# A channel-attention and MLP kernel: first chunk loaded without a cast, idle matmuls in the load stage, w_out prepared without GpSimd, and the batch change's reciprocal cut in four

## Chip, cores and metric

One core of one Trainium2 chip. The metric is the device time of one execution in microseconds (us).

## The reference

```
q, k, v: (4, 6080, 256) float32;  tau = 1
qn = q / (||q|| over the 6080 rows + 1e-6);  kn likewise
s  = kn^T @ qn / tau            # 256 x 256 for each of 4 batches
a  = softmax(s, last axis)
x  = (v @ a)                    # 24320 x 256
h  = x @ w_in                   # 256 -> 2048
y  = gelu_tanh(h) @ w_out       # 2048 -> 256
```

## The kernel before

A batch first needs its Gram matrix G = q^T k and the column norms, then a 256x256 softmax eT, then AW = a @ w_in (scaled by the row sums). From then on it is v-blocks of 512 rows: `hp = AW^T vT`, gelu on ScalarE (ACT), and the product with w_out. That product uses 7 instead of 8 half-size products on sums of weights and sums of gelu outputs; VectorE (DVE) makes the sums and TensorE (PE) accumulates them. The Gram matrix of the next batch is computed in between, pair by pair. For these later batches exp is made as (1 + tanh)/(1 - tanh), which is where the long reciprocal stands. Each block has eight pairs p = 0..7. Twelve blocks make a batch.

Names in the profile lines: `G` is the Gram matrix, `ss` a column sum of squares, `rk` and `dg` the factors 1/|k|, `S` the scaled scores, `eT` the softmax's numerators, `hp` and `g` a block's values before and after gelu, `wst` and `wcomb` w_out as loaded and as prepared, `r`, `p` and `q` accumulators of products, `c` a sum that DVE makes of two of them, `ot` the result that DVE transposes (its "turn"). An eviction is the copy of a finished product out of PE's accumulator. Code below is cut.

The load stage of batch 0 (all its q and k must be there before anything else can start):

```python
for c in range(nch):                     # chunks of 8, 7, 8, 8, 8, 6, 2 row groups
    if c >= 2:
        load_qk(0, c)                    # GpSimd queue, casts float32 to bf16
    if c >= 1:
        ss_rows(c - 1, 0); ss_rows(c - 1, 1)   # column sums of squares, on PE
    squares(0, c); fold_rows(0, c)       # ACT and DVE
    if c == nch - 1:
        ss_rows(c, 0); q_factor()
    for i in range(len(rows_of(0, c))):
        gram_row(0, c, i)
    if c == nch - 1:
        ss_rows(c, 1)
# ... loads of w_in, v, w_out ...
warm(14); scores(0); pe_vt(0, "r"); first_aw()   # idle matmuls, softmax, v transposed, AW
```

The weights' sums, in the first two blocks, and the loop at a batch change:

```python
def prep_wout(step):                     # step 0, 1 in block 0; 2 in block 1
    if step == 0:
        nc.gpsimd.tensor_copy(wc(A11), w_half(0, 0))
        nc.gpsimd.tensor_copy(wc(A12), w_half(0, 1))
        nc.gpsimd.tensor_scalar_mul(wc(NA22), w_half(1, 1), -1.0)
        nc.vector.tensor_add(WF[0], w_half(1, 0), w_half(1, 1))
        nc.vector.tensor_copy(wc(S1), WF[0])
        ...
# in the loop over blocks n and pairs p (cut):
    mm1(n, p)                            # hp and gelu
    mm2(n - 1, p)                        # products of the block before
    if p == 7: sums_2(n, 0, 4)           # three DVE sums
    if blk == 9:
        if p == 5: k_row(nxt)            # DVE: 1/norms, dg = diag(1/|k|)
        if p == 7: k_row_pe(nxt)         # PE: ones @ dg, then S on DVE
    if blk == 10:
        if p == 1: scores_b(nxt); scores_c(nxt)    # tanh; one 128x512 reciprocal; eT
        if p == 6: row_sums(nxt)                   # PE, reads eT
    if blk == 11:
        aw_part(nxt, p // 2, p % 2, "act" if p % 2 else "dve")
```

## Time and profile before

| | before |
|---|---|
| time, median of 3 runs | 727.25 us (726.23 to 728.44) |
| the profiled run | 728.82 us, span of the core 726.9 us |
| PE busy | 692.1 us |
| idle PE before 40 us / 40 to 75 / 75 to 700 / after | 16.2 / 3.5 / 9.4 / 5.8 us |
| first hp matmul | 41.45 us |

PE is busy 95% of the span.

### The profile page before, as it was taken

To read this page: it belongs to the slowest core of one execution; us is meant where nothing else is said; L and a number is where in the kernel's file an instruction comes from. 1 tells how busy PE (TensorE), PEld (TensorE's weight loads), DVE (VectorE), ACT (ScalarE), POOL (GpSimd) and SP (SyncE) were. 2 spreads that over 40 slices of the span, in tenths; PEclk is the share of its full clock that TensorE was granted. 3 is DMA by queue.
4 is the path that set the end of the run, shared out by engine and by line. 5 is a ranking of instruction groups with operands and counts; after the bars stand their busy time and mean duration, and the time that the engine had idled before them with its cause. 6 is when DMAs were issued, how large, how long until landed. Compare 5 with 4: busy or idle time off the path is not lost.

```text
span 726.9 us, 12069 instructions
## 1 busy us (share of the span) xinstructions
PE 692.1 (95%) x4752; PEld 469.7 (65%) x4840; DVE 509.0 (70%) x892; ACT 482.0 (66%) x589; POOL 76.5 (11%) x136
## 2 busy tenths in 40 slices
PE   4698999999999999999999999999999999999996
PEld 3555666666666666666666666666666666666665
DVE  3479787875866777788675878787686465564665
ACT  3275766776667667767666776677666767666673
POOL 4251101110001101110000110111000000000000
PEclk9899999999999999999999999999999999999999
DMA  9994897883349777875545887897334636556233
GB/s 175 201 249 78 134 138 115 134 133 57 59 67 156 116 130 136 137 109 87 86 73 83 140 139 121 124 143 115 57 60 72 99 59 99 77 80 94 42 59 55
DMA packets 161705, 77.87 MB, mean 107 GB/s; under 512 B 149408, under 2 KB 152736, under 8 KB 160928
## 3 DMA queue, kind: packets, MB, share of 16 engines
q0 software_dynamic: 14224, 40.51, 34.8%
q1 hardware_dynamic: 146944, 36.47, 31.0%
q8 instruction: 38, 0.62, 0.3%
q10 hardware_dynamic: 480, 0.11, 0.1%
q14 instruction: 19, 0.16, 0.1%
HBM read 78.91 MB, written 36.57 MB: 159 GB/s over the span
## 4 chain that ended last, share of the span: by engine, by line
PE 88%; DVE 5%; DMA 4%; issue 1%; ACT 1%; POOL 0%; DVEq 0%; POOLq 0%
PE hp L395 41%; PE r L489 23%; PE p L489 11%; PE q L489 5%; PE G L192 5%; DMA t<-in_k_dram 2%; PE ps L371 2%; DVE dn L348 1%; DMA t<-in_q_dram 1%; DVE c L505 1%; DVE aw L378 1%; DVE wf_a L442 1%; DVE t L460 0%; ACT th L340 0%; ACT g L399 0%
## 5 line engine op out<-in xcount | busy, mean ns | idle before, releaser
L399 ACT ACTIVATE g<-hp 128x1024 bf16<-128x1024 f32 (+1 forms) x384 | 387.9, 1015 | 203.9 <-PE hp L395 192.2
L395 PE MATMUL hp<-vT,aw 128*128 128x512 bf16 (+1 forms) x1363 | 354.4, 376 | 2.6
L489 PEld LDWEIGHTS <-wcomb 128*128 128x128 bf16 x2688 | 262.8, 98 | 107.1 <-issue 9.1
L395 PEld LDWEIGHTS <-aw 128*128 128x128 bf16 x1536 | 149.9, 98 | 109.0 <-issue 1.7
L489 PE MATMUL r<-t,wcomb 128*128 128x256 bf16 (+1 forms) x1152 | 148.6, 272 | 7.1 <-DVE c L505 6.8
L192 PE MATMUL G<-t 128*128 128x256 bf16 (+1 forms) x384 | 71.3, 289 | 14.6 <-DMA t<-in_k_dram 14.6
L505 DVE TENSOR_TENSOR c<-r,y 128x256 f32<-128x256 f32 (+1 forms) x95 | 39.9, 420 | 50.9 <-PE r L489 46.8
L505 DVE TENSOR_TENSOR c<-q,x 128x256 f32<-128x256 f32 (+1 forms) x48 | 20.2, 420 | 72.7 <-PE q L489 70.9
L473 DVE TENSOR_TENSOR t<-t,g 128x1024 bf16<-128x1024 bf16 (+1 forms) x96 | 65.0, 677 | 0.0
L472 DVE TENSOR_TENSOR t<-g 128x1024 bf16<-128x1024 bf16 (+1 forms) x96 | 64.9, 676 | 0.0
L471 DVE TENSOR_TENSOR t<-g,t 128x1024 bf16<-128x1024 bf16 (+1 forms) x96 | 63.4, 660 | 0.0
L111 POOL DMA_DIRECT2D vb<-in_v_dram x45 | 22.8, 507 | 356.3 <-PE hp L395 356.3
L513 DVE STREAM_TRANSPOSE ot<-c 128x256 f32<-128x256 f32 (+1 forms) x144 | 57.6, 425 | 1.9 <-DVE c L505 0.2
L144 ACT ACTIVATE sq<-t 128x1536 bf16<-128x1536 bf16 (+3 forms) x30 | 45.6, 1520 | 19.7 <-DMA t<-in_q_dram 16.6
L460 DVE TENSOR_TENSOR t<-g 128x2048 bf16<-128x2048 bf16 (+1 forms) x48 | 57.7, 1203 | 0.0
L192 PEld LDWEIGHTS <-t 128*128 128x128 bf16 (+1 forms) x384 | 39.3, 103 | 27.4 <-issue 10.2
L489 PE MATMUL r<-g,wcomb 128*128 128x256 bf16 (+1 forms) x384 | 49.3, 271 | 1.2
L489 PE MATMUL p<-t,wcomb 128*128 128x256 bf16 (+1 forms) x384 | 49.3, 271 | 1.1 <-DVE wcomb L443 1.1
L489 PE MATMUL p<-g,wcomb 128*128 128x256 bf16 (+1 forms) x384 | 49.3, 271 | 0.0
L489 PE MATMUL q<-g,wcomb 128*128 128x256 bf16 (+1 forms) x384 | 49.3, 271 | 0.0
L513 DVE STREAM_TRANSPOSE ot<-r 128x256 f32<-128x256 f32 (+1 forms) x48 | 21.4, 445 | 29.7 <-PE r L489 29.7
L145 DVE TENSOR_TENSOR sq<-t 128x1536 bf16<-128x1536 bf16 (+4 forms) x31 | 29.8, 961 | 15.0 <-DMA t<-in_k_dram 14.7
(95 smaller groups left out, 332.8 us busy)
## 6 DMA issues: line engine op xcount, KB each, us to landing
out_dram<-ot SPq DMA_DIRECT2D x176, 128.0 KB, 2.9
vb<-in_v_dram POOLq DMA_DIRECT2D x41, 256.0 KB, 5.2
t<-in_q_dram POOLq DMA_DIRECT2D x22, 384.0 KB, 5.2
t<-in_k_dram POOLq DMA_DIRECT2D x22, 384.0 KB, 4.4
t<-in_q_dram POOLq DMA_DIRECT2D x4, 512.0 KB, 12.5
t<-in_k_dram POOLq DMA_DIRECT2D x4, 512.0 KB, 13.5
wst<-in_moe_w_out_dram POOLq DMA_DIRECT2D x2, 1024.0 KB, 10.0
out_dram<-ot SPq DMA_DIRECT2D x12, 112.0 KB, 2.6
```

The costliest lines, as they stand in the source:

```text
L144: nc.scalar.activation(sq[:, 0:n, 0:256], qt[:, 0:n, :], AF.Square)
L145: nc.vector.tensor_mul(sq[:, 0:n, 256:512], kt[:, 0:n, :], kt[:, 0:n, :])
L192: nc.tensor.matmul(G[b][:, jc, :], lhsT=qt[:np_, r, jc * 128 : jc * 128 + 128], rhs=kt[:np_, r, :], start=first and jc == 0, stop=last and ...
L395: mm = nc.tensor.matmul(hp[:, u, :cols], lhsT=AW[b][:, cc, fc * 128 : fc * 128 + 128], rhs=vt_tiles[n][:, cc, :cols], start=cc == 0, stop= ...
L399: nc.scalar.activation(GS[n][:, 2 * p : 2 * p + 2, :cols], hp[:, :, :cols], AF.Gelu_apprx_tanh)
L460: nc.vector.tensor_sub(t1[:, :, :hc], quarter(n, 0, 1), quarter(n, 0, 0))
L471: nc.vector.tensor_sub(v[2], b22, v[1])
L472: nc.vector.tensor_sub(v[3], b22, quarter(n, 0, 1, f0, f1))
L473: nc.vector.tensor_sub(v[4], v[2], quarter(n, 1, 0, f0, f1))
L489: nc.tensor.matmul(ACCS[n, acc][:, :hc], lhsT=wcomb[:, w, fc, :], rhs=x, start=first and fc == 0, stop=fc == 7, skip_group_check=True)
L505: nc.vector.tensor_add(CS[n][:, tj, ci, :hc], ACCS[n, acc][:, :hc], XS[n, name][:, :hc])
L513: nc.vector.transpose(OT[n][:, tj * nb : tj * nb + nb, ci, :], src.rearrange("p (x t) -> p x t", t=32))
```

## The change

The intent is to shorten every place where PE waits: start the load earlier by two hardware queues, keep the clock up during the load, take the preparation of w_out off GpSimd (while GpSimd works on it, a DVE sum takes 3.78 instead of 1.21 us), and cut the one long reciprocal so that DVE can serve PE in between. The transposes of v's first block also move ahead of the softmax. The diff is cut.

```diff
+    def load_first():           # q by the SP queue, k by the ACT queue, float32, no cast
+    def cast_first(st):         # q cast on ACT, k on DVE
-        load_qk(0, 0)
+        first = load_first()
         load_qk(0, 1)
+        load_qk(0, 2)
+        WARM = [0, 6, 10, 12, 14, 14, 0]
+            if 1 <= c < nch - 1:
                 ss_rows(c - 1, 0)
                 ss_rows(c - 1, 1)
+                warm(WARM[c])                       # idle matmuls
-        warm(14); scores(0); pe_vt(0, "r"); first_aw()
+        pe_vt(0, "r"); warm(14); scores(0); first_aw()   # both vT copies now on DVE
+                if (f, ic) == (0, 1): nc.scalar.activation(o, i, AF.Copy, scale=...)
-            nc.gpsimd.tensor_copy(wc(A11), ...)  (and A12, NA22)
+            nc.vector.tensor_copy(wc(A11), w_half(0, 0))
+        if step == 2: nc.scalar.activation(wc(A12), w_half(0, 1), AF.Copy)
+        if step == 3: nc.scalar.activation(wc(NA22), w_half(1, 1), AF.Copy, scale=-1.0)
     def scores_c(b, step):      # four pieces of 128x128; eT behind the fourth
+        nc.vector.reciprocal(piece, piece)
                     if blk == 9:
-                        if p == 5:
+                        if p == 7:
                             k_row(nxt)
-                        if p == 7:
-                            k_row_pe(nxt)
                     if blk == 10:
+                        if p == 0:
+                            k_row_pe(nxt)
                         if p == 1:
                             scores_b(nxt)
-                            scores_c(nxt)
-                        if p == 6:
+                        if p in (2, 4, 6, 7):
+                            scores_c(nxt, (2, 4, 6, 7).index(p))
+                    if blk == 11:
+                        if p == 0:
                             row_sums(nxt)
-                        aw_part(nxt, p // 2, p % 2, "act" if p % 2 else "dve")
+                        aw_part(nxt, p // 2, p % 2, "act" if p in (1, 4, 5, 6) else "dve")
```

More of the change, by code (lines that the diff above doesn't have):

```diff
@@ L98, in load_one @@
         qk_tiles.setdefault((b, c), []).append(t)
+    def load_first():
+        r0, n = chunks_of(0)[0]
+        assert not with_rest(0, 0)
+        st = gp.tile([128, 2, n, 256], FP32, tag="g", name="qk_f32")
+        for which, eng in ((0, nc.sync), (1, nc.scalar)):
+            eng.dma_start(out=st[:, which], in_=(q, k)[which][0, 0 : R * 128, :].rearrange(
+                "(p r) c -> p r c", r=R)[:, r0 : r0 + n, :])
+        return st
+    def cast_first(st):
+        for which in range(2):
+            t = qkp.tile([128, 8, 256], BF16, tag="qk"[which], name=f"first{which}")
+            for h in range(2):
+                if which == 0:
+                    nc.scalar.activation(t[:, h * 4 : h * 4 + 4], st[:, 0, h * 4 : h * 4 + 4], AF.Copy)
+                else:
+                    nc.vector.tensor_copy(t[:, h * 4 : h * 4 + 4], st[:, 1, h * 4 : h * 4 + 4])
+            qk_tiles.setdefault((0, 0), []).append(t)
     def load_qk(b, c):
@@ L267, in pe_vt @@
         nc.vector.tensor_copy(vT[:, 0, :], ps[:, 0, :])
-        if n == 0:
-            nc.scalar.activation(vT[:, 1, :], ps[:, 1, :], AF.Copy)
-        else:
-            nc.vector.tensor_copy(vT[:, 1, :], ps[:, 1, :])
+        nc.vector.tensor_copy(vT[:, 1, :], ps[:, 1, :])
         vt_tiles[n] = vT
@@ L292, in first_aw @@
             for ic in range(2):
-                nc.vector.tensor_scalar_mul(AW[b][:, ic, f * 256 : f * 256 + 256],
-                                            ps[ic][:, f * 256 : f * 256 + 256], rs[:, ic : ic + 1])
+                o = AW[b][:, ic, f * 256 : f * 256 + 256]
+                i = ps[ic][:, f * 256 : f * 256 + 256]
+                if (f, ic) == (0, 1):
+                    nc.scalar.activation(o, i, AF.Copy, scale=rs[:, ic : ic + 1])
+                else:
+                    nc.vector.tensor_scalar_mul(o, i, rs[:, ic : ic + 1])
     def warm(n):
@@ L341, in scores_b, with scores_c @@
         TH[b] = th
-    def scores_c(b):
-        th = TH.pop(b)
-        dn = smx.tile([128, 2, 256], FP32, tag="S")
-        nc.vector.tensor_scalar(dn, th, -1.0, 1.0, op0=ALU.mult, op1=ALU.add)
-        nc.vector.reciprocal(dn, dn)
-        eT = smx.tile([128, 2, 256], BF16, tag="eT")
-        nc.vector.scalar_tensor_tensor(eT, th, 1.0, dn, op0=ALU.add, op1=ALU.mult)
-        ET[b] = eT
+    def scores_c(b, step):
+        th = TH[b]
+        if step == 0:
+            dn = smx.tile([128, 2, 256], FP32, tag="S")
+            DN[b] = dn
+            nc.vector.tensor_scalar(dn, th, -1.0, 1.0, op0=ALU.mult, op1=ALU.add)
+        dn = DN[b]
+        piece = dn[:, step // 2, step % 2 * 128 : step % 2 * 128 + 128]
+        nc.vector.reciprocal(piece, piece)
+        if step == 3:
+            eT = smx.tile([128, 2, 256], BF16, tag="eT")
+            nc.vector.scalar_tensor_tensor(eT, th, 1.0, dn, op0=ALU.add, op1=ALU.mult)
+            ET[b] = eT
+    DN = {}
     def row_sums(b):
@@ L438, in prep_wout @@
                 WF.append(t)
-            nc.gpsimd.tensor_copy(wc(A11), w_half(0, 0))
-            nc.gpsimd.tensor_copy(wc(A12), w_half(0, 1))
-            nc.gpsimd.tensor_scalar_mul(wc(NA22), w_half(1, 1), -1.0)
+            nc.vector.tensor_copy(wc(A11), w_half(0, 0))
             nc.vector.tensor_add(WF[0], w_half(1, 0), w_half(1, 1))
@@ L448, in prep_wout @@
         if step == 2:
+            nc.scalar.activation(wc(A12), w_half(0, 1), AF.Copy)
+        if step == 3:
+            nc.scalar.activation(wc(NA22), w_half(1, 1), AF.Copy, scale=-1.0)
+        if step == 4:
             nc.vector.tensor_sub(wc(S3), w_half(0, 0), w_half(1, 0))
@@ L618 @@
         nch = len(chunks_of(0))
+        WARM = [0, 6, 10, 12, 14, 14, 0]
         for c in range(nch):
-            if c >= 2:
+            if c == 0:
+                cast_first(first)
+            if c >= 3:
                 load_qk(0, c)
-            if c >= 1:
+            if 1 <= c < nch - 1:
                 ss_rows(c - 1, 0)
                 ss_rows(c - 1, 1)
+                warm(WARM[c])
             squares(0, c)
             fold_rows(0, c)
+            if c == nch - 2:
+                ss_rows(c, 0)
             if c == nch - 1:
@@ L629 @@
                 q_factor()
+                ss_rows(c - 1, 1)
             for i in range(len(rows_of(0, c))):
@@ L642 @@
         load_v0(2)
+        pe_vt(0, "r")
         warm(14)
         scores(0)
-        pe_vt(0, "r")
         first_aw()
@@ L660 @@
                 gate = mm1(n, p)
+                if n == 1 and p in (0, 3):
+                    prep_wout(2 + p // 3)
                 if p == 0 and n + 3 < NN:
@@ L673 @@
                         if n == 1:
-                            prep_wout(2)
+                            prep_wout(4)
                     if p == PAIRS - 1:
@@ L698 @@
                             norms(nxt)
-                        if p == 5:
+                        if p == 7:
                             k_row(nxt)
-                        if p == 7:
+                    if blk == 10:
+                        if p == 0:
                             k_row_pe(nxt)
-                    if blk == 10:
                         if p == 1:
                             scores_b(nxt)
-                            scores_c(nxt)
-                        if p == 6:
+                        if p in (2, 4, 6, 7):
+                            scores_c(nxt, (2, 4, 6, 7).index(p))
+                    if blk == 11:
+                        if p == 0:
                             row_sums(nxt)
-                    if blk == 11:
-                        aw_part(nxt, p // 2, p % 2, "act" if p % 2 else "dve")
+                        aw_part(nxt, p // 2, p % 2, "act" if p in (1, 4, 5, 6) else "dve")
         mm2_last(NN - 1)
```

## The prediction

> **What bounds the kernel now.** I first read the page's busy line, then who PE waits for, then the granted clock in short stretches, then the timelines of PE and DVE around each wait.
>
> ```profile
> PE 692.1 (95%) x4752; PEld 469.7 (65%) x4840; DVE 509.0 (70%) x892; ACT 482.0 (66%) x589; POOL 76.5 (11%) x136
> ```
>
> TensorE is busy 692.1 of 726.9 us, and the change removes no TensorE work of size. So all it can win lies in the 35 us of idle time and in stretches at half clock. By the table of stretches, 16.2 us of the idle time lies before 40 us, 3.5 us between 40 and 75 us, 9.8 us between 75 and 700 us, 5.8 us in the tail. The waits of PE:
>
> ```profile
> PE G L192 <- DMA t<-in_k_dram: 14.6, 4, 8.9
> PE r L489 <- DVE c L505: 6.8, 10, 1.9
> PE ss L210 <- DVE a L156: 1.6, 3, 0.7
> PE p L489 <- DVE wcomb L443: 1.1, 1, 1.1
> ```
>
> The first row is the load of q and k: the softmax of batch 0 needs all 12.5 MB, and the DMA engines show a share of about 1.0 from 4 us on. The second row has ten waits: one of 1.94 us at 64.49 us, and 0.33 + 0.87 + 0.42 = 1.62 us at each of three batch changes (183.83, 196.36, 211.58 us and their repeats); 1.94 + 3 x 1.62 = 6.8. The row of 1.1 is the wait for the summed weights at 54.77 us. The clock, in stretches of 3.41 us:
>
> ```profile
> 21.28:24.70 3.42, 2.00 (x24) 1.66 (x23) 1.22 (x1) 1.65 (x1) 1.45 (x2) 1.00 1.07 214
> 24.70:28.11 3.41, 1.42 (x18) 0.90 (x16) 1.23 (x1) 1.91 (x1) 0.70 (x1) 1.00 1.06 211
> 28.11:31.52 3.41, 2.05 (x10) 1.43 (x10) 1.94 (x2) 0.19 (x1) 0.71 (x1) 0.50 1.06 207
> ...
> 62.25:65.66 3.41, 1.47 (x16) 1.17 (x15) 3.28 (x6) 1.68 (x2) 0.53 (x1) 1.00 0.47 53
> 65.66:69.07 3.41, 3.41 (x17) 1.88 (x15) 2.87 (x7) 0.77 (x1) 0.00 (x0) 0.50 0.34 67
> ```
>
> The second column is PE's busy time, the third from the end the granted clock. A stretch with 1.42 or 1.47 us busy is followed by one at 0.50, one with 2.00 us busy is not. So the wait of 1.94 us is paid twice: the half clock after it costs about 3.41 / 2 = 1.7 us. What DVE does before these two waits:
>
> ```profile
> 49.71 3.78 DVE L442 TENSOR_TENSOR wf_a<-wst,wst 128x1024 f32<-128x1024 f32 x1
> 53.53 1.18 DVE L443 CAST wcomb<-wf_a 128x1024 bf16<-128x1024 f32 x1
> 54.63 1.21 DVE L444 TENSOR_TENSOR wf_a<-wf_a,wst 128x1024 f32<-128x1024 f32 x1
> ...
> 57.02 0.68 DVE L447 CAST wcomb<-wf_a 128x1024 bf16<-128x1024 f32 x1
> ```
>
> The same sum takes 3.78 us while GpSimd works on w_out (49.34 to 54.16 us) and 1.21 us alone, and the same cast 1.18 against 0.68. DVE then runs full until 65 us.
>
> **What the Trainium skill says.** (1) "SBUF — State Buffer", section "Who interferes with whom": a DVE instruction with two SBUF inputs contends with a GpSimd instruction that reads SBUF, and whoever comes first holds the pair for its whole instruction. The trace agrees (3.78 against 1.21). (2) "TensorE: Matmul & The Clock Gate", Part 1: the clock is halved or full, decided over free-running windows of 3413 ns. The length agrees: full speed ends at 28.11 and 65.66 us, 11 x 3.413 apart. The page asks for an idle window; here a window that was 42% busy was enough. (3) "DMA: Bandwidth & Descriptors", Specifications: first byte after about 0.6 us by hardware queue, 1 us by software queue; no run yet shows the first here. The "Key Constraints" of "Trainium Kernel Development and Optimization" say that all queues share the same 16 engines, so the new queues add no bandwidth. (4) "VectorE: DVE Perf Modes", "First, the fixed hardware budget": reciprocal is an iterative divide. The trace: 128x512 in 3.35 us and 128x4 in 0.18, so 6.24 ns an element; four pieces cost about what one does.
>
> **Part 1, the load.** The casting loads write 205 GB/s of bf16, which is 410 GB/s read; the fp32 loads of w_out at 42 to 47 us ran at 320 to 379 GB/s. So 2.1 MB of first chunk without the cast takes 5.8 instead of 5.1 us, 0.7 us more. Against it stands the start: between 2 and 4 us only 61 and 106 GB/s were written, 1.2 us worth of full rate lost, and the first issue waited for GpSimd until 1.23 us. I give 1.3 us back. The load ends about 0.6 us earlier. The first chunk itself lands later (three queues share the engines) and needs a cast, but PE has time to spare: chunks arrive every 5 us and need 3 to 4 us of work.
>
> **Part 2, idle matmuls.** They keep the clock full at 28 to 35 us, which alone would gain about 1 us at the last chunks. But they cost PE time where it counts: the fold of chunk 4 ends at 32.04, its sums end at about 32.75, 14 idle matmuls (0.109 us each, 1.53) end at 34.28, chunk 5's 12 Gram matmuls at 35.9, the rest about 37.5. Before, all of it ended at 37.60. So this part gives 0.1 us, and with Part 1 the head gains 0.7 us. The AW eviction on ScalarE gives nothing: the first hp starts at 41.45 us, when PE has just finished the ps matmuls (40.59 to 41.47), not when DVE has.
>
> **Part 3, w_out.** DVE now does A11 (0.68), the sum (1.21), S1 (0.68), the difference (1.2): S1 is ready at 49.75 + 2.6 = 52.3 instead of 54.7, before PE asks at 53.7. That removes 1.07 us. All of DVE's later work moves 2.4 us earlier. ScalarE takes A12 and -A22, 1.0 us each by the gelu of the same size (1.02); it has 0.6 to 0.9 us free per pair there and PE does not wait for it. At the product that waited 1.94 us PE now arrives 1.07 earlier and DVE 1.9 earlier (the sum is at 62.15 instead of 64.4, less the ends of pipelines): about 0.7 us of wait stay, PE is then 80% busy in that window, and the half clock goes. Gain: 1.07 + 1.24 + 1.7 = 4.0 us.
>
> **Part 4, batch changes.** Here I step through both engines in program order with the durations of the trace (hp 0.87, a product 0.87, three sums of half a block 1.77, c 0.34, L460 1.14). What goes: 0.33 (the k row no longer between two c), 0.87 (the long reciprocal), 0.42 (the AW eviction at p = 4 goes to ScalarE). What comes:
>
> ```profile
> 185.28 0.65 DVE L471 TENSOR_TENSOR t<-g,t 128x1024 bf16<-128x1024 bf16 x1
> 185.85 0.68 DVE L472 TENSOR_TENSOR t<-g 128x1024 bf16<-128x1024 bf16 x1
> 186.45 0.69 DVE L473 TENSOR_TENSOR t<-t,g 128x1024 bf16<-128x1024 bf16 x1
> ```
>
> These three stand at the end of every block, right behind the turn of r. The k row moves behind them: turn 0.37, sums 1.77, k row 0.87, some 0.2 of latency, 3.2 us after product 4; PE needs 3 x 0.87 = 2.6 to reach the matmul that reads it. A new wait of 0.6 to 0.7. One block later the fourth piece (0.9) and eT (0.7) stand behind the same sums: 0.4 + 0.37 + 1.77 + 0.9 + 0.7 = 4.1 us after product 4, and the row sums, moved to p = 0 of the next block, are reached after 2.6. A new wait of 1.5. Sum per batch change: 0.7 + 1.5 - 1.62 = +0.6, three times +1.8 us. A stall of 1.5 us leaves a window at least 56% busy, beside the 58% that did not drop and the 43% that did; I allow 0.3 us in all for a lost clock.
>
> **Sum:** -0.7 - 4.0 + 1.8 + 0.3 = -2.6, so 727.25 becomes 724.6 us.
>
> **Rivals.** (a) The batch changes work as meant: all 1.62 us go, three times, and the new waits do not come, because DVE does the sums or the pieces faster than I add up. For it: DVE is idle 0.6 us before the k matrices in my schedule. Against it: program order is fixed, and eT stands behind the sums. Then -0.7 - 4.0 - 4.9, 717.6 us. (b) The new wait of 1.5 us drops the clock each time: +1.7 three times, about 729.5. For it: the threshold lies between 43 and 58% of a window. Against: the wait must fall wholly into one window. (c) The DMA bounds the head and the hardware queues slow it (0.7 us more and a poorer start), and DVE stays the bound behind w_out with the clock still dropping: only 1.5 of the 4.0 come, 728.5.
>
> **Range and chances.** The stages are independent: head -1.5 to +0.7, w_out -5 to -2, batch changes -4 to +5. The low end 719.5 takes most of (a), the high end 729.0 is (b) or (c) nearly whole. 2% is 14.5 us; the whole removable idle time named here is 1.07 + 1.94 + 1.7 + 4.9 = 9.6 us, so faster by 2% has 0.01, and slower by 2% 0.01.
>
> **What would show it.** Right: no wait for wcomb and under 1 us for c at 60 to 70 us with the clock at 1.00; the 128x1024 sum at 1.2 us; new rows of PE waiting for dg (0.7, three times) and for eT at the row sums (1.5, three times); rows of c at batch changes gone; hp starting at 40.5 to 41.3 us. Wrong: no wait at the row sums (Part 4 fails), half clock at 190 to 205 us (b), first hp later than 41.5 us or half clock at 60 to 70 us (c).

## The result, and the profile after

726.11 us (median of 4 runs, 725.94 to 726.32) beside 726.79 us for the kernel before (4 runs, 726.23 to 728.44). Ratio 0.9987, 95% interval 0.997 to 1.0005: the same. Ratios here are the mean time of one kernel's fast runs over that of the other's of the same rounds, so they are not quite the ratio of the medians. The profiled run took 726.32 us, its span 724.6 us. The busy line of the page, and then who PE waits for (total us, times, longest us):

```profile
PE 693.5 (96%) x4808; PEld 472.0 (65%) x4896; DVE 508.8 (70%) x904; ACT 486.0 (67%) x593; POOL 70.2 (10%) x131
```

```profile
PE ps L386 <- DVE eT L377: 4.4, 3, 1.5
PE ps L350 <- DVE dg L344: 1.8, 3, 0.6
...
PE r L520 <- DVE c L536: 0.7, 1, 0.7
PE vt_ps L285 <- DMA v<-in_v_dram: 0.5, 1, 0.5
```

The ten waits for c (6.8 us) and the one for wcomb (1.1 us) have become one of 0.7 us. In their place stand three for eT and three for dg, one of each at each batch change. Stretches of the new trace around 65 us, columns as in the prediction:

```profile
58.81:62.22 3.41, 2.71 (x19) 1.70 (x18) 3.38 (x6) 3.41 (x5) 0.53 (x1) 1.00 0.22 43
62.25:65.66 3.41, 3.31 (x31) 2.48 (x30) 2.97 (x7) 1.59 (x2) 0.00 (x0) 1.00 0.78 115
65.66:69.07 3.41, 3.22 (x21) 1.93 (x21) 3.34 (x7) 2.25 (x3) 0.51 (x1) 1.00 0.07 12
```

The wait of 0.7 us that is left ends at 61.95 us and so falls into the first of them, which is still 79% busy. The second holds 3.31 us of busy time where before held 1.47 in the same stretch, and the clock stays at 1.00. DVE's timeline during the w_out sums:

```profile
50.22 1.22 DVE L469 TENSOR_TENSOR wf_a<-wst,wst 128x1024 f32<-128x1024 f32 x1
51.48 0.69 DVE L470 CAST wcomb<-wf_a 128x1024 bf16<-128x1024 f32 x1
```

These were 3.78 and 1.18 us. Adding up the two traces, by the starts of the same PE instructions:

| stage | before | after | difference |
|---|---|---|---|
| start to first hp | 41.45 | 41.40 | -0.05 |
| first hp to the first hp of block 2 | 29.28 | 25.38 | -3.90 |
| from there to the first product of 224 columns (first batch change in it) | 146.51 | 147.37 | +0.86 |
| from one such product to the next (second; the third alike) | 172.24 | 172.81 | +0.57 |
| the same product in the last batch to the end | 11.39 | 11.05 | -0.34 |

The sum, with the third batch change, is -2.3, which is what the two spans differ by. Of the +0.86, 0.30 us lie at the very start of block 2, where its first product follows the first hp after 1.16 us instead of 0.86; so w_out brings -3.6, and the first batch change costs 0.56 like the others. So w_out and the batch changes did roughly what the prediction said, the head did not, and in the two profiled runs the whole is -2.5 us of device time against a forecast of -2.6. Yet the medians differ by 0.7 only. Two questions are left: why the medians show less, and how much of this is really due to each part.

### The profile page after: what moved, and what is told of

It is laid out like the page before. It is cut to its first block, busy times and chain, and to the rows that moved or that the text cites. A ratio compares the mean times of both kernels' runs of the same rounds, so it can differ in the third digit from the quotient of the medians.

```text
span 724.6 us, 12205 instructions
## 1 busy us (share of the span) xinstructions
PE 693.5 (96%) x4808; PEld 472.0 (65%) x4896; DVE 508.8 (70%) x904; ACT 486.0 (67%) x593; POOL 70.2 (10%) x131
## 3 DMA queue, kind: packets, MB, share of 16 engines
q10 hardware_dynamic: 624, 1.16, 0.5%
## 4 chain that ended last, share of the span: by engine, by line
PE 87%; DVE 6%; DMA 4%; issue 1%; POOL 1%; ACT 0%; DVEq 0%; POOLq 0%
PE hp L424 41%; PE r L520 22%; PE p L520 11%; PE q L520 6%; PE G L213 4%; DMA t<-in_k_dram 2%; DMA v<-in_v_dram 2%; PE ps L400 2%; DVE ot L544 1%; DVE dn L374 1%; DVE t L504 1%; DVE t L502 1%; DVE t L503 1%; DVE c L536 0%; POOL t L93 0%
## 5 line engine op out<-in xcount | busy, mean ns | idle before, releaser
L213 PE MATMUL G<-t 128*128 128x256 bf16 (+1 forms) x368 | 64.8, 273 | 1.1 <-DMA t<-in_k_dram 1.1
L165 ACT ACTIVATE sq<-t 128x1536 bf16<-128x1536 bf16 (+3 forms) x29 | 43.7, 1506 | 9.8 <-DMA t<-in_q_dram 9.8
L213 PEld LDWEIGHTS <-t 128*128 128x128 bf16 (+1 forms) x368 | 35.5, 98 | 11.2 <-issue 2.7
L529 ACT ACTIVATE y<-p 128x256 f32<-128x256 f32 (+1 forms) x95 | 36.3, 382 | 0.7 <-ACT x L529 0.4
```

Source lines behind the costliest of these rows:

```text
L165: nc.scalar.activation(sq[:, 0:n, 0:256], qt[:, 0:n, :], AF.Square)
L213: nc.tensor.matmul(G[b][:, jc, :], lhsT=qt[:np_, r, jc * 128 : jc * 128 + 128], rhs=kt[:np_, r, :], start=first and jc == 0, stop=last and ...
L529: nc.scalar.activation(x[:, :hc], ACCS[n, acc][:, :hc], AF.Copy)
```

## The experiments

The parts were cut out of the diff and put on the kernel before one at a time (e1 to e3), or taken back from the changed kernel (e6, e7), and the batch changes were reordered (e4).

### e1: only w_out

```diff
-            nc.gpsimd.tensor_copy(wc(A11), w_half(0, 0))   # and A12, NA22
+            nc.vector.tensor_copy(wc(A11), w_half(0, 0))
+        if step == 2: nc.scalar.activation(wc(A12), w_half(0, 1), AF.Copy)
+        if step == 3: nc.scalar.activation(wc(NA22), w_half(1, 1), AF.Copy, scale=-1.0)
```

> The kernel before with the w_out part alone (A11 on DVE, A12 and -A22 on ScalarE, none on GpSimd). Theory: the waits of 1.07 and (1.94 - 0.70) us go, 2.3 us, and 1.7 us more in those runs of before that have a half-clock stretch at 65 us; so 722.9 to 724.5 beside 726.8. Rival, given back later: the time is within 0.7 us of before, with new PE waits after 75 us.

724.96 us (724.27 to 725.25, 6 runs) beside 726.3 (725.79 to 730.31, 11 runs); ratio 0.9964 (0.994 to 0.9988). This is a gain of 1.3 us by the medians, short of the 2.3 us that the theory asked for at the least. The rival fails too: it asked for less than 0.7 us and for new waits later. Why less than the 2.3 us of waits? In this run the clock was full at the last chunks, the first hp came at 39.98 us instead of 41.45, and DVE then had to wait for w_out itself:

```profile
49.28 1.23 DVE L440 TENSOR_TENSOR wf_a<-wst,wst 128x1024 f32<-128x1024 f32 x1 [0.39 <-DMA wst<-in_moe_w_out_dram]
```

From the first hp to that of block 2 it takes 25.87 us, beside 25.38 in the changed kernel and 27.44 in e2, which has the old w_out code and no half clock there. So against a full clock this part gains 1.6 us, not the 3.6 of the two profiled runs.

### e2: only the batch changes

```diff
  kernel before, with scores_c in four steps and the loop's lines for blk 9, 10, 11 taken from the change
```

> The kernel before with the batch-change part alone (k row later, reciprocal in four pieces, row sums a block later, AW evictions split differently). Theory: at each of three batch changes waits of 0.60 (dg) and 1.47 (eT) come and 1.62 go, so +0.45 to +0.6 each, 728.1 to 728.6 beside 726.8. Rival, pieces help as meant and the loss seen in the trace comes from the rest of the change: 722 to 725.

727.77 us (727.51 to 730.91, 6 runs): five of the six runs lie at 727.5 to 728.0. Beside the same runs of before as e1 that is 1.5 us more by the medians; the ratio, 1.0013 (0.9983 to 1.0042), has an interval that takes in 1, because before's mean holds its slower runs. The rival (722 to 725 us) failed. The trace has the same waits as the whole change (eT 4.4, dg 1.8 us) and 172.80 us from one product of 224 columns to the next, against 172.24 before. The loss at the batch change belongs to this part, not to the rest of the change.

This trace also settles something else. It still has the old w_out code and so the wait at 62 us, 1.95 us long, but no half clock follows it. PE's timeline, then the stretches between two window boundaries (its own clock returned to full at 27.5 us; 61.62 and 65.03 are 10 and 11 times 3.413 us later):

```profile
62.71 1.03 PE L496 MATMUL r<-t,wcomb 128*128 128x256 bf16 x8 [1.95 <-DVE c L512]
```

```profile
61.62:65.03 3.41, 2.32 (x22) 1.81 (x22) 2.97 (x6) 0.53 (x1) 0.00 (x0) 1.00 0.78 120
58.20:61.62 3.42, 2.56 (x17) 1.56 (x16) 3.39 (x7) 2.78 (x3) 0.53 (x1) 1.00 0.59 103
```

The wait lies across a boundary. Each window keeps 68 to 75% of busy time, and none is answered by half clock. In the profiled run of before the same wait lay inside one window (43% busy) and cost 1.8 us more: first hp to block 2 took 27.44 us here and 29.28 there. e3, which keeps the old w_out code too, agrees: its wait of 1.9 us leaves the two windows that it touches 79 and 64% busy, and the clock stays at 1.00.

### e3: only the head

```diff
  kernel before, with load_first, cast_first, the chunk loop, WARM, the vT order and the AW eviction taken from the change
```

> The kernel before with everything of the change up to the first hp (hardware-queue load, idle matmuls, vT of block 0 before the softmax, one AW eviction on ScalarE). Theory: last sums end 0.9 us earlier, but the vT copies stand before S on DVE and give all of it back; first hp at 41.4 us, time within 0.4 us of before. Rival: the head is worth the 0.7 us that the whole change gained, 726.1.

726.8 us (726.5 to 727.76, 6 runs), ratio 0.9994 (0.997 to 1.0019). The first hp came at 40.96 us, better than foreseen and yet 0.9 to 1.0 us later than in e1 and e2, which have the old head. By the medians it is 0.5 us slower than before, a little outside the 0.4 us of the theory; the rival's 726.1 did not come. So the head is no gain over an old head with full clock.

### e4: batch changes reordered

```diff
-                        if p == 7:
+                        if p == 6:
                             k_row(nxt)
-                        if p in (2, 4, 6, 7):
-                            scores_c(nxt, (2, 4, 6, 7).index(p))
+                        if p in (2, 3, 4, 6):
+                            scores_c(nxt, (2, 3, 4, 6).index(p))
```

> The changed kernel with the k row one pair earlier (p = 6, ahead of the block's last sums) and the reciprocal's pieces at p = 2, 3, 4, 6 instead of 2, 4, 6, 7, so that eT too stands ahead of those sums. Theory, only the order on DVE is at fault: the waits for dg (3 x 0.60) and eT (3 x 1.47) go, 6.2 us, 719.9 beside 726.1. Rival, DVE is short of time there whatever the order: the waits move to c or to the product that reads the half-block sums, 723 or more.

718.28 us (718.08 to 718.53, 6 runs), ratio to before 0.9874 (0.985 to 0.9897): 1.6 us below the theory, and far from the rival. Not one wait for eT or dg is left in PE's list of waits. In the changed kernel DVE's timeline behind the turn of r, at the end of block 10, was this:

```profile
196.68 0.68 DVE L504 TENSOR_TENSOR t<-t,g 128x1024 bf16<-128x1024 bf16 x1
197.28 0.94 DVE L374 RECIPROCAL dn<-dn 128x128 f32<-128x128 f32 x1
198.25 0.69 DVE L377 SCALAR_TENSOR_TENSOR eT<-th,dn 128x512 bf16<-128x512 f32 x1
```

PE's row sums in that trace:

```profile
199.00 0.25 PE L386 MATMUL ps<-ones_bf,eT 128*128 128x1 bf16 x4 [1.47 <-DVE eT L377]
```

In e4, the same work stands ahead of the turn and the sums, on DVE and then on PE:

```profile
192.79 0.91 DVE L374 RECIPROCAL dn<-dn 128x128 f32<-128x128 f32 x1
193.74 0.69 DVE L377 SCALAR_TENSOR_TENSOR eT<-th,dn 128x512 bf16<-128x512 f32 x1
194.35 0.44 DVE L544 STREAM_TRANSPOSE ot<-r 128x256 f32<-128x256 f32 x1
```

```profile
195.80 0.24 PE L386 MATMUL ps<-ones_bf,eT 128*128 128x1 bf16 x4
```

eT is ready 1.4 us before PE asks for it. DVE does as much as before the move (904 instructions, 508.0 and 508.8 us busy), so it was not short of time there; only its order was wrong. The gain is larger than the 6.2 us of waits: from one product of 224 columns to the next it takes 170.31 us instead of 172.81, 2.5 us for each batch change and 7.5 in all. The list of waits gives 2.07 for each because it counts from a matmul's modelled end; from start to start the two places cost 1.63 and 2.50 us with the wait and 0.88 each without, 2.37 in sum.

### e5: the kernel before kept warm

```diff
+                if n == 1 and p == 5:
+                    warm(14)
```

> The kernel before with 14 idle matmuls (1.5 us) in the wait of 1.94 us at 62.5 us, nothing else. Before's runs fall into two groups, 725.8 to 727.1 and 729.0 to 730.3. Theory: the slow group is the half-clock stretch that follows this wait when a clock window happens to cover it; kept busy, PE never gets it, so all six runs lie below 727.5 and the median at 726.0 to 726.5. Rival, the slow group comes from the half clock in the load stage (before 40 us): two or so of six runs stay at 729 to 730.

726.3 us (725.78 to 728.08, 6 runs) beside 726.62 (725.83 to 728.92, 11 runs). No run lies at 729, where before has two of eleven. But two runs, 727.69 and 728.08, are outside what the theory allowed. The profile of the first shows why:

```profile
27.80:31.21 3.41, 1.64 (x8) 1.13 (x8) 1.53 (x2) 0.16 (x1) 0.71 (x1) 0.52 1.06 208
31.21:34.63 3.42, 3.42 (x25) 2.44 (x23) 2.36 (x4) 1.48 (x1) 1.47 (x2) 0.50 1.18 182
62.00:65.41 3.41, 3.00 (x27) 2.35 (x26) 3.38 (x6) 1.91 (x2) 0.53 (x1) 1.00 0.41 52
```

The clock is full at 62 us, but half over the last chunks, and the first hp comes at 41.43 us instead of the 39.98 and 40.10 of e1 and e2. There are thus two places where the position of the windows decides: the load stage (about 1.4 us) and the wait at 62 us (about 1.8 us). Together they make 3.2 us; two runs of before at 730.3, 4.2 above the common group, need something more, which no trace shows. Nor does the mean clock tell the runs of e5 apart (0.993 or 0.994 in all six): what counts is where the half clock falls. The rival was half right. Over the three calls with clocks recorded, 21 of 29 runs of before have a mean clock of 0.993 or more and lie at 725.8 to 727.2 us (median 726.1); the other eight, at 0.990 to 0.992, lie at 728.0 to 730.3. With six runs here, the absence of a slow one is consistent with the theory and no proof; the two traces of e2 and of before are the stronger evidence.

### e6: v's transposes back behind the softmax

```diff
-        pe_vt(0, "r"); warm(14); scores(0)
+        warm(14); scores(0); pe_vt(0, "r")
```

> The changed kernel with the transposes of v's first block back behind the softmax's instructions. Theory: in the changed kernel S waits on DVE for the two vT copies, which wait for the load of v, 0.85 us; so 0.6 to 0.9 us faster than the changed kernel of the same rounds, first hp at about 40.5 us. Rival, the idle matmuls ahead of the AW matmuls set the start: no difference.

725.41 us (725.06 to 726.43, 6 runs), against 725.88 for the changed kernel in the same rounds (e8): 0.5 us faster, a little under the theory. First hp at 40.21 us. The changed kernel, DVE ahead of S, the softmax's first step (ACT had rk ready at 37.7):

```profile
37.88 0.42 DVE L288 COPY vT_pe<-vt_ps 128x512 bf16<-128x512 bf16 x1 [3.67 <-PE vt_ps L285]
38.22 0.41 DVE L289 COPY vT_pe<-vt_ps 128x512 bf16<-128x512 bf16 x1
38.55 0.75 DVE L267 TENSOR_TENSOR S<-G,rk 128x256 f32<-128x256 f32 x2
```

and e6:

```profile
37.35 0.75 DVE L267 TENSOR_TENSOR S<-G,rk 128x256 f32<-128x256 f32 x2 [3.56 <-ACT rk L263]
```

In e8, the changed kernel in the same rounds, S started at 37.78 us and the first hp came at 40.63; so e6 has both 0.4 us earlier. S waits for rk again and no longer for the load of v. The order of PE's stream (pe_vt ahead of the idle matmuls) and of DVE's (copies ahead of S) had put a transfer on the path that had been off it.

### e7: no idle matmuls between the chunks

```diff
-        WARM = [0, 6, 10, 12, 14, 14, 0]
+        WARM = [0] * 7
```

> The changed kernel without the idle matmuls between Gram chunks (the 14 ahead of the softmax stay). Theory: with a full clock in the last chunks it starts up to 1 us earlier, as the 14 idle matmuls before chunk 5 cost 1.5 us on PE; with a half clock there it starts up to 1 us later; so a median within 0.7 us of the changed kernel and a spread of the runs over 1 us where the changed kernel has 0.4. Rival, they are needed: all runs slower by about 1 us.

726.22 us (725.78 to 726.34, 6 runs), 0.3 us above e8. The spread did not grow to over 1 us (0.56), so that part of the theory missed. In its trace the last sums start at 35.50 us, against 35.85 in e8, although chunk 4 ran at half clock; then the transposes wait 1.1 us for v (36.98 us; 0.2 us in e8), which the order of the change puts on the path. The idle matmuls hide behind that wait; alone this run decides nothing about them. e10 and e11 do.

### e8: the changed kernel again

> The changed kernel again, on the chip and in the rounds of the three others, as their base. Expected 726.1, spread under 0.6 us, since no half-clock stretch is left in it; against the fast group of before no difference of more than 0.5 us, against its slow group 3 to 4 us.

725.88 us (725.54 to 726.56, 6 runs), ratio 0.9986 (0.9972 to 1.0000). Together with the first four runs: ten of ten at 725.5 to 726.6, a spread of 1.0 where 0.6 was expected, median 726.0. Against the common group of before (726.1) that is 0.1 us; against the rare group (728.0 to 730.3) it is about 3 us. What the change bought is mostly that the rare group is gone: ten runs are few, but their mean clocks, 0.998 to 1.000, say the same.

### e9 to e12: putting it together

```diff
  e9:  e4 + e6
  e10: e9 with WARM = [0] * 7
  e11: e9 with WARM = [0, 6, 10, 12, 14, 0, 0]
  e12: kernel before + w_out part + batch changes as in e4 (old head)
```

> The mended batch changes (718.3 alone) and v's transposes behind the softmax (0.5 us alone): if the two stages are independent, 717.8; if the earlier start only meets a later wait (the w_out weights or the load of the next operand), 718.3.

> As e9 without the idle matmuls between Gram chunks. Theory: the 14 ahead of chunk 5 cost 1.5 us of PE and a half clock costs about 1 us, in those runs where it falls late; the median 0.3 to 0.9 us below e9, with a wider spread. Rival, the idle matmuls earn their place: 0.5 us or more above e9.

> As e9 with the idle matmuls up to chunk 4 but not the 14 ahead of chunk 5: full clock and no queue behind them. Theory: the best of the three, last sums at 35.0 to 35.4 us instead of 36.3, 717.0. Rival, the load of v or of w_in then sets the start: no better than e9.

> The kernel before with the w_out part and the mended batch changes, but the head as it was. Batch changes lose 3 x 1.62 us of waits against before, w_out 1.5 to 2: so 719.5 in runs with full clock at the last chunks, 1.4 more with half clock there; that tells what the new head adds to a kernel that is otherwise the same (e4: 718.3).

| 4 runs each | median us | range | first hp, us |
|---|---|---|---|
| before (7 runs) | 726.18 | 725.98 to 728.89 | |
| e9 | 717.80 | 717.53 to 718.00 | 40.28 |
| e10 | 717.38 | 717.24 to 717.86 | 39.36 |
| e11 | 716.66 | 716.51 to 716.97 | 39.56 |
| e12 | 718.61 | 718.44 to 719.97 | 40.49 |

e9 came out as expected. e10 lies 0.4 us below it, as its theory had it, and e11 1.1 us below. Both confirm the cost of the last 14 idle matmuls: PE's timeline of e9 and of e11 ahead of chunk 5's Gram matmuls,

```profile
31.71 1.69 PE L322 MATMUL warm<-zeros_bf,ones_bf 128*128 128x256 bf16 x14
33.24 0.44 PE L231 MATMUL ss<-ones_bf,sq 128*128 128x1 bf16 x12
33.54 1.47 PE L213 MATMUL G<-t 128*128 128x256 bf16 x12
```

```profile
32.11 0.45 PE L231 MATMUL ss<-ones_bf,sq 128*128 128x1 bf16 x12
32.43 1.47 PE L213 MATMUL G<-t 128*128 128x256 bf16 x12
```

Chunk 5 starts 1.1 us earlier, and the time is 1.1 us less by the medians (in the two profiled runs the first hp and the span gain 0.7). The last sums of e11 start at 34.92 us (36.04 in e9), just ahead of the range foreseen. The rival for e11 is half true: its transposes wait 0.3 us for v. Why e11 is 0.7 us faster than e10 is not shown: in the profiles e10's first hp is even 0.2 us earlier. e11, ratio to before 0.9859 (0.9835 to 0.9883), 9.5 us by the medians, is the best version. With the old head the same kernel (e12) takes 718.61, so the head as the change has it, vT order mended (e9), is worth 0.8 us, and 2.0 us without the 14 idle matmuls. e12 itself lies 0.9 us below the 719.5 expected: that had counted 1.62 us of waits for a batch change, and the mended one saves 1.93 from product to product (172.24 - 170.31), 0.9 more in three.

## Why the prediction was right, and where it was not

**The total.** 726.11 lies in the range 719.5 to 729.0, and "within 2%" held. The point, 724.6, forecast a gain of 2.6 us; by the medians of the first rounds it was 0.7. The forecast was made against a trace that was itself of the slower group (728.82 us, clock 0.991). Between the two profiled runs the difference is 2.5. That this is so close to 2.6 is partly luck: the head fell 0.65 short there, the 0.3 set aside for the clock was not needed, and 0.34 came at the very end, where the forecast had nothing. Against a full clock the stages sum up otherwise (an estimate from the traces): the head +0.5 (40.63 us in e8 beside 40.10 in e2), w_out -2.1 (25.38 beside 27.44), batch changes +1.7. That is about 0, and the medians of e8 and of the common group of before differ by 0.2. (In the prediction, 9.8 us of idle time between 75 and 700 us should be 9.4; nothing rests on it.)

**Part 4, batch changes: right in sign, place and size.** Forecast: waits of 0.6 to 0.7 for dg and 1.5 for eT, together +0.6 at each change. Measured: 0.60, 1.47, and +0.57 from product to product; alone (e2) +1.5 us by the medians. Rival (a), that the waits would not come, failed, and e4 shows that it would have been possible: one pair earlier for the k row and for the last pieces turns +1.7 into -5.8 us (3 x 1.93). Here the prediction's 1.62 us, read from the waits, was too small by 0.31.

**Rival (b), a lost clock at the new waits: did not come.** The changed kernel's runs have mean clocks of 0.998 to 1.000. The 0.3 us allowed for it were not needed.

**Part 3, w_out: right for the profiled run, too large for a typical one.** The term of 1.7 us for the half clock was taken as a property of the kernel. It is a property of where the windows lie in one execution: the wait of 1.94 us cost it in the profiled run of before and not in e2's or e3's. The other terms held in the changed kernel's trace: no wait for wcomb, 0.7 us of wait for c left, 1.22 us for the sum. On an old head with full clock (e1) even they are smaller, since PE then reaches this stage earlier and the load of w_out becomes the wait.

**Parts 1 and 2, the head: the step that failed.** The prediction let the head gain 0.7 us. The result of its Part 1 held (the two terms, +0.7 and -1.3, were not seen apart): the first bytes came between 1 and 2 us instead of 2 and 3, the first chunk moved at 401 to 410 GB/s at 3 to 6 us without the cast, and chunks 4 and 5 were there 0.75 us earlier (28.70 and 32.38 us instead of 29.45 and 33.12), where 0.6 had been forecast. The last sums began at 36.32 us instead of 37.22. But the first hp came at 41.40. The step that failed is silent in the text: nothing was worked out for moving v's transposes ahead of the softmax. They waited for v (0.5 us), and their two DVE copies stood in front of S, which started at 38.55 instead of 37.7 us; e6 puts the cost at 0.4 to 0.5 us. How much of it one run meets varies: in e8 v came sooner and the first hp at 40.63, inside the range foreseen. The second half of the failure is the yardstick: the gain was counted from a first hp of 41.45, after a half clock over the last chunks. With a full clock there the old head needs 39.98 and 40.10 us (e1, e2), so the new one is later by 0.5 us or more. Likewise "they keep the clock full ... But they cost PE time where it counts", with 0.1 left, was right against a half clock; against the full clock that most runs of before, by their times, have there, the last 14 idle matmuls are a loss of 1.1 us (e11 beside e9).

**What was read wrongly in the first place.** The half clock at 28 to 35 us and at 66 to 69 us of one trace was taken for the kernel's normal run. The three times given with that trace (726.23 to 728.44) and its own 728.82 said otherwise.

What stays open: the parts are not additive by the medians (e1 -1.3, e2 +1.5, e3 +0.5 us, sum +0.7, whole -0.7). The load of w_out, which the early start of e1 runs into, accounts for 0.5 us of that (25.87 beside 25.38 us). Beside the common group of before alone the whole is -0.1 to -0.2, so most of the rest would lie in how many slower runs each median of before holds; that is argued and not shown.

## What to carry to other kernels

Cutting a long instruction into pieces helped here only when each piece, and above all the result behind the last one, stood in its engine's program order ahead of work that nobody waits for; write down the order on the engine, not the pairs it is "spread over". A half-clock stretch in one trace may be luck of that run: look at the spread of the times and at each run's mean clock before counting on winning it back. Idle matmuls that keep a clock up belong where PE would wait anyway, not ahead of the last work that the next stage waits for.

## What the Trainium skill lacked or had wrong

- "TensorE: Matmul & The Clock Gate", Part 1 and its advice table, put the fall to half clock down to an idle window and to gaps over some 3 us; the section "A second HAM failure mode" has short idles suffice in another kernel, without saying how much. Here a wait of 1.94 us was enough when it lay inside one 3.41 us window (1.47 us busy, 43%; also 1.42 us, 42%), windows with 2.00 us (58%) and more kept the clock, and the same wait across two windows (68 and 75% busy, e2) brought no half clock. No sharp line comes out: windows in the load stage, placed by each run's own changes of clock, with 1.66 us (e10) and 1.72 us busy (e5) lost it, with 1.65 (e10), 1.71 (e2) and 1.78 us (e1) kept it. The page says that the window is free-running and that the count of slow matmuls at a kernel's start varies with it, but not that the times of a long kernel can fall into groups for it: 725.8 to 727.2 and 728.0 to 730.3 us here.
- "DMA: Bandwidth & Descriptors", "Where 436 GB/s comes from", says that for HBM to SBUF the HBM side binds at about 358 GB/s. Only its section on measured bandwidth adds that this is with both cores of a pair streaming. With one core, the first chunk and the casting loads beside it moved 401 to 410 GB/s at 3 to 6 us, which fits the 425 GB/s measured there for one core.
- "VectorE: DVE Perf Modes" tells that reciprocal is an iterative divide and gives no time for it. Here: 3.35 us for 128x512, 0.91 to 0.95 us for 128x128, about 6.2 ns for each element of a partition.
